# A written-out order of 1,498 words for a hash-attention and MLP kernel: PSUM banks dealt as the score tiles are made, and the order remade from unit 3's scores on

## The chip, the cores and the metric

One core of one Trainium2 chip. The metric is device time in microseconds (us) of one execution. The kernel before took 294.7 us, the median of three runs (295.97, 294.70 and 294.19).

## What is computed

Attention over 4 batches, 8 heads, 768 positions of 64 numbers, in which a query sees only the keys of its own hash bucket; then a layer norm and a two-matrix MLP with a residual over rows of 512.

```python
q_bits = (einsum('bhsd,dk->bhsk', q, proj) > 0)      # 6 bits for a query, the same for a key
q_bucket = sum(q_bits * powers, axis=-1)
mask = q_bucket[:, :, :, None] == k_bucket[:, :, None, :]
scores = where(mask, scale * matmul(q, k.transpose(0, 1, 3, 2)), -1e9)
attn = softmax(scores)
x = matmul(attn, v).transpose(0, 2, 1, 3).reshape(B, S, H * D)
xn = (x - mean) / sqrt(var + 1e-06) * g_ln
out = x + maximum(xn @ w_ch1, 0.0) @ w_ch2
```

## The kernel before, in words

The work is cut into 12 units of 256 query rows, three for each batch (unit u belongs to batch u // 3), and each unit into two halves g of four heads.

**A list of words sets the order.** ORDER (line 16) holds 1,498 words such as `S.t.7.1.0`: an operation, an engine (t TensorE, v VectorE, a ScalarE, p GpSimd, s the DMA queue of SyncE), and its place. Line 911 runs through the list and calls for each word the function of that name, so each engine does its words in the order in which they stand, and waits in line where an operand isn't there. Nothing reorders them later. The words that the prediction speaks of:

- `S.t.u.g.k` (S_, line 596) is a score word: 12 matmuls for keys k of unit u, half g, in three rounds (hash bits, then the two halves of q and k), on four groups of 32 rows at once. Six words, k = 0 to 5, make six tiles of two banks each: words 0 to 2 make tiles a = 0, words 3 to 5 tiles a = 1. With the first word of three come the tiles p = 0 and 1, with the second p = 2 and the rest of p = 1, with the third the rest of p = 0 and 2. So p = 1 is complete after the words k = 0 and 1 (3 and 4), p = 0 after k = 0 and 2 (3 and 5), p = 2 after k = 1 and 2 (4 and 5).
- `E.a.u.g.a.p` (line 622) is the exponential of one such tile on ScalarE, 1024 numbers a partition; it gives the tile's banks back. `A.t.u.g.a.p` (line 627) multiplies it with V into a tile acc, which `na.v` (line 644) reads.
- `sv.a.u.t` (line 672) is ScalarE's sum of squares of a row block for the layer norm, `ce.v.u.t` (line 685) centres and scales it, `fl.s.u.t` (line 704) turns it by a transposing DMA.
- The MLP's first matrix is `F.t.u.p` with `R` as its relu (units 0 to 3 and 11), or for units 4 to 10 seven products `M.t.u.p.h` (line 776) whose partial sums are copied by `V` (line 796) and added by `U` (line 807) or `Q` (line 811). The second matrix is `P.t.u.k` (line 872) in seven products, and `Y.v` adds each to x. `O.s` (line 890) writes x out.
- `mw.s` and `mr.s` (line 570) write the hash bits of a batch's half to DRAM and read them back as rows of G, which the score words take.

**Banks are dealt by a table.** PSUM has six banks for score and acc tiles, in three pairs (tag `pp`), and two for everything else (tag `f`). Each tile takes, when it is made, the next figure of a string in SLOTS (line 167) as the number of its slot; line 267 does it:

```python
def ps(name, shape, tag, dt=F32):
    if name not in made:
        n = taken.get(tag, 0)
        taken[tag] = n + 1
        tags[name] = f"{tag}_{SLOTS[tag][n]}"
        made[name] = psum.tile(shape, dt, name=name, tag=tags[name])
    return made[name]
```

A tile in a slot waits until the last reader of the tile before it in that slot is done. SBUF tiles (tags E, X, x and others) are dealt in the same way by `sb` (line 256).

Of the kernel before, what the change touches and what calls it, by code (L numbers as in the profile page):

```python
# [81 lines left out]
Y.v.3.7 hm.t.3.0 bt.v.3.0 S.t.6.0.3 N.a.6.0.1 S.t.6.0.4 E.a.6.0.1.1 bs.v.4.1 bs.v.4.3 bs.v.4.2 S.t.6.0.5
mr.s.2.1.3 E.a.6.0.1.2 O.s.2.0 sp.t.2.0 sc.v.2.0 mr.s.2.1.2 LX.s.3.1.0 mr.s.2.1.1 P.t.3.4 Y.v.3.4 M.t.4.1.0
V.v.4.1.0 E.a.6.0.1.0 M.t.4.2.0 U.v.4.1.0 mw.s.3.0 S.t.6.1.0 O.s.3.0 N.a.6.1.0 w1s.v.4.0 M.t.4.6.0 sv.a.5.1
M.t.4.5.0 V.v.4.5.0 S.t.6.1.1 bs.v.4.4 V.a.4.6.0 M.t.4.7.0 U.v.4.4.0 M.t.4.3.0 sv.a.5.0 E.a.6.1.0.1 S.t.6.1.2
E.a.6.1.0.0 U.v.4.2.0 M.t.4.4.0 Q.v.4.0 rs.p.5 A.t.6.0.1.1 tu.v.3.1.0.0 ce.v.5.1 M.t.4.1.1 A.t.6.0.1.2
A.t.6.0.0.1 M.t.4.2.1 V.a.4.1.1 U.v.4.1.1 E.a.6.1.0.2 tu.v.3.1.0.3 A.t.6.0.0.0 M.t.4.6.1 V.a.4.6.1 lv.s.3.0.2
lv.s.3.4.0 LX.s.3.1.1 O.s.3.3 lv.s.3.0.1 A.t.6.0.1.0 A.t.6.0.0.2 na.v.6.0 O.s.3.2 M.t.4.5.1 ru.v.4.1 fl.s.5.1
M.t.4.7.1 S.t.6.1.4 S.t.6.1.3 ce.v.5.0 V.a.4.5.1 U.v.4.4.1 M.t.4.3.1 U.v.4.2.1 N.a.6.1.1 E.a.6.1.1.1 S.t.6.1.5
E.a.6.1.1.0 M.t.4.4.1 Q.v.4.1 mr.s.3.0.0 P.t.4.1 E.a.6.1.1.2 ru.v.4.4 ru.v.4.2 ss.v.4.1 P.t.4.2 fl.s.5.0  # L90
lv.s.3.0.3 S.t.7.0.0 N.a.7.0.0 S.t.7.0.1 S.t.7.0.2 E.a.7.0.0.1 E.a.7.0.0.0 Y.v.4.2 Y.v.4.1 P.t.4.5 O.s.2.2
ss.v.4.2 O.s.3.1 ss.v.4.4 ss.v.4.3 bs.v.5.1 Y.v.4.5 P.t.4.6 tu.v.3.1.1.0 A.t.6.1.0.0 Y.v.4.6 A.t.6.1.0.1
A.t.6.1.0.2 nb.v.6.0 E.a.7.0.0.2 P.t.4.3 Y.v.4.3 lv.s.3.4.3 P.t.4.7 A.t.6.1.1.0 A.t.6.1.1.2 sp.t.2.4
A.t.6.1.1.1 sc.a.2.4 Y.v.4.7 P.t.4.4 M.t.5.1.0 tu.v.3.1.1.3 bs.v.5.2 na.v.6.1 mr.s.3.0.1 Y.v.4.4 S.t.7.0.3
tu.v.3.1.0.2 lv.s.3.4.2 bs.v.5.3 V.a.5.1.0 N.a.7.0.1 tu.v.3.1.0.1 S.t.7.0.4 E.a.7.0.1.1 M.t.5.2.0 U.v.5.1.0
S.t.7.0.5 E.a.7.0.1.2 E.a.7.0.1.0 M.t.5.6.0 M.t.5.5.0 S.t.7.1.0 V.v.5.6.0 N.a.7.1.0 M.t.5.7.0 S.t.7.1.2
V.a.5.5.0 S.t.7.1.1 nb.v.6.1 mn.p.6 E.a.7.1.0.0 sv.a.6.1 lv.s.3.4.1 O.s.4.1 bs.v.5.4 M.t.5.3.0 U.v.5.4.0
M.t.5.4.0 O.s.2.3 mr.s.3.0.3 Q.a.5.0 A.t.7.0.0.1 A.t.7.0.1.2 U.v.5.2.0 A.t.7.0.1.1 M.t.5.1.1 E.a.7.1.0.1
M.t.5.2.1 on.p.3 A.t.7.0.0.0 A.t.7.0.0.2 E.a.7.1.0.2 tu.v.3.1.1.1 A.t.7.0.1.0 V.v.5.1.1 M.t.5.6.1 U.v.5.1.1
na.v.7.0 M.t.5.5.1 O.s.4.0 S.t.7.1.3 tu.v.3.1.1.2 V.a.5.6.1 M.t.5.7.1 V.a.5.5.1 ru.a.5.1 M.t.5.3.1 U.v.5.4.1  # L100
N.a.7.1.1 sv.a.6.0 S.t.7.1.4 S.t.7.1.5 E.a.7.1.1.1 E.a.7.1.1.0 E.a.7.1.1.2 U.v.5.2.1 rs.p.6 M.t.5.4.1 ru.v.5.4
Q.v.5.1 ru.v.5.2 hm.t.3.1 P.t.5.2 S.t.8.0.0 N.a.8.0.0 S.t.8.0.1 ss.v.5.1 E.a.8.0.0.1 ce.v.6.1 ss.v.5.3
bt.v.3.1 fl.s.6.1 S.t.8.0.2 E.a.8.0.0.0 E.a.8.0.0.2 nb.v.7.0 P.t.5.1 cv.a.3.4.0 A.t.7.1.0.1 A.t.7.1.1.2
Y.v.5.2 Y.v.5.1 ss.v.5.2 ce.v.6.0 A.t.7.1.0.2 A.t.7.1.0.0 A.t.7.1.1.1 A.t.7.1.1.0 na.v.7.1 nb.v.7.1 mn.p.7
P.t.5.6 Y.v.5.6 S.t.8.0.3 N.a.8.0.1 S.t.8.0.4 E.a.8.0.1.1 S.t.8.0.5 ss.v.5.4 E.a.8.0.1.0 P.t.5.5 P.t.5.7
bs.v.6.3 E.a.8.0.1.2 Y.v.5.5 P.t.5.3 su.v.3.0 S.t.8.1.0 N.a.8.1.0 sv.a.7.1 S.t.8.1.1 S.t.8.1.2 E.a.8.1.0.2
Y.v.5.3 sp.t.3.0 Y.v.5.7 sc.v.3.0 P.t.5.4 sv.a.7.0 rs.p.7 fl.s.6.0 M.t.6.1.0 mw.s.3.1 mr.s.3.1.2 cv.v.3.0.0
A.t.8.0.1.2 A.t.8.0.0.0 Y.v.5.4 V.v.6.1.0 O.s.4.3 A.t.8.0.0.1 bs.v.6.1 M.t.6.2.0 bs.v.6.2 E.a.8.1.0.1
# [63 lines left out]
    X="012302312031201001",  # L172
# [14 lines left out]
    x="012301320132",  # L187
    xnT="010101010101",
)

@with_exitstack
def kernel(
    ctx: ExitStack,
# [750 lines left out]
```

## Time and profile before

| | |
|---|---|
| runs shown | 295.97, 294.70, 294.19 us; median 294.70 |
| the profiled execution, its own time | 293.72 us |
| its span in the trace | 292.0 us (1.7 us lie around it) |
| granted TensorE clock | 1.00 |
| TensorE matmuls busy | 280.4 us, 96% of the span |
| VectorE, ScalarE, GpSimd busy | 244.8, 228.9, 32.9 us |
| exponentials on ScalarE | 144 of 1.11 us, 152.2 us |

The trace names a tile without its numbers (sc for every score tile). "Releaser" is what ended the idle time before an instruction. A matmul's bar reaches some 0.17 us beyond the start of the next one, since matmuls are pipelined, so short waits do not show as idle time; the distance from the start of one word to the start of the next shows them.

### The profile page before, as it was taken

The numbers are of one execution on the slowest core, as the hardware profiler recorded it, in microseconds if no ns is written. First come the engines' busy times: TensorE is split into PE (matmuls) and PEld (weight loads), VectorE is DVE, ScalarE is ACT, GpSimd is POOL, SyncE is SP. The second block draws the span as 40 slices with busy tenths as digits, with TensorE's granted clock in tenths as the row PEclk, the third lists the DMA queues.
The fourth block names the chain that finished last, engine by engine and source line by source line (L and its number), as shares of the span: only waits on it lengthen the run. The fifth ranks groups of instructions, "written<-read, shape, count | busy, mean of one in ns | idle before, by whom it ended". The sixth has DMA issues, their size and how long they took to land.

```text
span 292.0 us, 11314 instructions
## 1 busy us (share of the span) xinstructions
PE 280.4 (96%) x4924; PEld 228.0 (78%) x4927; DVE 244.8 (84%) x587; ACT 228.9 (78%) x285; POOL 32.9 (11%) x83
## 2 busy tenths in 40 slices
PE   8998999999999999999998999899999999999993
PEld 5777767558887886877886878698788789998882
DVE  5758899899998989898997899797997997998552
ACT  4889999999999859879847989898897896664240
POOL 4560500110003002001000102000101011010000
PEclk9999999999999999999999999999999999999999
DMA  6999999268752560444942012500042202003233
GB/s 205 362 293 270 217 278 173 58 203 225 203 159 75 135 225 2 111 146 106 205 140 60 4 38 57 114 11 2 12 101 56 57 3 55 24 0 56 53 93 91
DMA packets 31059, 34.15 MB, mean 117 GB/s; under 512 B 15521, under 2 KB 27809, under 8 KB 31010
## 3 DMA queue, kind: packets, MB, share of 16 engines
q1 hardware_dynamic: 25938, 28.72, 35.4%
q0 software_dynamic: 4224, 4.19, 8.7%
q8 instruction: 38, 0.62, 0.9%
q10 hardware_dynamic: 848, 0.53, 0.7%
q14 instruction: 11, 0.09, 0.1%
HBM read 27.86 MB, written 6.88 MB: 119 GB/s over the span
## 4 chain that ended last, share of the span: by engine, by line
PE 84%; DVE 7%; ACT 6%; issue 1%; DVEq 0%; ACTq 0%
PE sc L606 17%; PE X L880 12%; PE acc L634 11%; PE f L725 10%; PE Ma L791 7%; PE Yb L880 6%; ACT E L623 4%; PE Ya L880 3%; PE Me L791 3%; PE hp L550 3%; PE hf L418 3%; PE f L828 2%; PE Mb L791 2%; PE warm L388 1%; DVE T L329 1%
## 5 line engine op out<-in xcount | busy, mean ns | idle before, releaser
L623 ACT ACTIVATE E<-sc,bias_sb 128x1024 bf16<-128x1024 f32 x144 | 152.2, 1112 | 17.8 <-PE sc L606 17.2
L606 PE MATMUL sc<-qb,kb 32*128 32x256 bf16 x1152 | 52.4, 267 | 0.0
L606 PE MATMUL sc<-G 6*128 6x256 bf16 (+1 forms) x576 | 43.0, 272 | 3.2 <-ACT E L623 3.1
L634 PE MATMUL acc<-vaug,E 128*128 128x65 bf16 x1152 | 43.1, 193 | 0.4 <-ACT E L623 0.4
L634 PEld LDWEIGHTS <-E 128*128 128x128 bf16 x1152 | 40.5, 97 | 2.1 <-issue 1.0
L725 PE MATMUL f<-xnT,w_sb 128*128 128x256 bf16 x320 | 38.8, 273 | 0.4 <-ACT hb L733 0.2
L880 PEld LDWEIGHTS <-hb 128*128 128x128 bf16 x352 | 33.0, 98 | 7.3 <-issue 3.1
L725 PEld LDWEIGHTS <-w_sb 128*128 128x128 bf16 x320 | 30.2, 98 | 5.4 <-issue 2.1
L606 PEld LDWEIGHTS <-kb 32*128 32x128 bf16 x1152 | 30.6, 93 | 1.2
L606 PEld LDWEIGHTS <-G 6*128 6x128 bf16 (+1 forms) x576 | 17.4, 91 | 17.2 <-issue 12.4
L733 ACT ACTIVATE hb<-f 128x512 bf16<-128x512 f32 x33 | 19.6, 599 | 13.5 <-PE f L725 10.5
L880 PEld LDWEIGHTS <-S 128*128 128x128 bf16 x264 | 25.2, 98 | 4.3 <-issue 1.1
L329 DVE STREAM_TRANSPOSE T<-X 128x384 f32<-128x384 f32 (+2 forms) x52 | 26.6, 539 | 0.0
L885 DVE TENSOR_TENSOR x<-X,x 128x256 f32<-128x256 f32 x44 | 18.3, 418 | 5.8 <-PE X L880 5.6
L880 PE MATMUL Yb<-w_sb,S 128*128 128x256 bf16 x176 | 22.8, 273 | 0.0
L791 PEld LDWEIGHTS <-w_sb 128*128 128x128 bf16 x336 | 20.2, 97 | 3.0 <-issue 2.8
L880 PE MATMUL X<-wt,hb 128*128 128x256 bf16 x168 | 21.8, 273 | 0.0
L791 PEld LDWEIGHTS <-Wx 128*128 128x128 bf16 x336 | 19.6, 98 | 2.3 <-issue 2.1
L646 DVE SCALAR_TENSOR_TENSOR y<-vsB,acc 128x520 f32<-128x520 f32 x24 | 16.6, 690 | 5.0 <-PE acc L634 4.8
L669 POOL TENSOR_TENSOR rw<-rw 128x2 f32<-128x2 f32 x9 | 2.1, 237 | 139.1 <-DVE x L659 139.1
L791 PE MATMUL Ma<-bs,Wx 128*128 128x128 bf16 x192 | 14.7, 219 | 0.0
L659 DVE SCALAR_TENSOR_TENSOR x<-y,rc 128x256 f32<-128x256 f32 x36 | 13.9, 422 | 0.6
(134 smaller groups left out, 441.4 us busy)
## 6 DMA issues: line engine op xcount, KB each, us to landing
out_dram<-x SPq DMA_DIRECT2D x45, 128.0 KB
X<-in_k_dram SPq DMA_DIRECT2D x7, 768.0 KB
vn<-in_v_dram SPq DMA_DIRECT2D x24, 192.0 KB
X<-in_q_dram SPq DMA_DIRECT2D x6, 768.0 KB
w_sb<-in_moe_w_ch_dram POOLq DMA_DIRECT2D x8, 512.0 KB, 12.5
vn<-in_v_dram SPq DMA_DIRECT2D x2, 768.0 KB
X<-in_q_dram SPq DMA_DIRECT2D x2, 512.0 KB
Bd<-B SPq DMA_DIRECT2D x6, 96.0 KB
```

Of the source, the lines that this page charges most:

```text
L329: nc.vector.transpose(d[:, j], s[:, j, kj0 : kj0 + n])
L418: nc.tensor.matmul(hf(g, t, kp)[:, :256], pfull[:, j], tp(g, t, kp)[:, j], start=(j == 0), stop=(j == 1))
L606: m = nc.tensor.matmul(sc(u, g, a, p)[:, bank, 256 * half : 256 * half + 256], lh, rh, start=(rep == 0), stop=(rep == 2), skip_group_check ...
L623: nc.scalar.activation(Ep(u, g, a, p), sc(u, g, a, p), AF.Exp, scale=EXP_SCALE, bias=bias_sb)
L634: nc.tensor.matmul(acc[:, qt, (D + 1) * i : (D + 1) * (i + 1)], Ep(u, g, a, p)[:, bank, 256 * half + P * qt : 256 * half + P * qt + P], va ...
L646: nc.vector.scalar_tensor_tensor(yt(u, g), vs, EPS_ROW, made[f"acc{u}_{g}"][:, :, :A], op0=AOP.mult, op1=AOP.add,)
L659: nc.vector.scalar_tensor_tensor(xo[:, t], a[:, t, :, 0:D], 1.0, rc[:, t].to_broadcast([P, 4, D]), op0=AOP.mult, op1=AOP.mult, accum_out=r ...
L725: nc.tensor.matmul(f1[:, n].rearrange("p (t x) -> p t x", t=2), w1_sb[:, dt, P * nt : P * nt + P], xnT(u)[:, :, dt], start=(dt == 0), stop ...
L733: nc.scalar.activation(hb(u)[:, 2 * p : 2 * p + 2], f1, AF.Relu)
L791: nc.tensor.matmul(m[:, n], lh(kt)[:, P * nt : P * nt + P], rh[:, kt], start=(first and n == 0 and kt == 0), stop=(kt == 1), skip_group_ch ...
L880: nc.tensor.matmul(f2, lh[:, n], rh[:, n], start=(first and n == 0), stop=(n == 7), skip_group_check=True)
L885: nc.vector.tensor_tensor(x, made[f"{prod(u, k)}{u}"], x, op=AOP.add)
```

## The change

The first 299 words stay. From the scores of unit 3 on the list is another: the same work in another sequence, with 44 words on another engine (ScalarE or VectorE; seen over all, 304 words stand on ScalarE before and 300 after, 454 and 458 on VectorE; TensorE and SyncE have the same words, 550 and 144). Five strings of SLOTS change with it: pp, f, E, X and x. No function changes, and no arithmetic. "Measured times of the squares" is a note on how the new list was made (the durations of sv); it has no line in the code.

One line of the list and the string of the score banks, before and after:

```diff
-A.t.6.1.1.1 sc.a.2.4 Y.v.4.7 P.t.4.4 M.t.5.1.0 tu.v.3.1.1.3 bs.v.5.2 na.v.6.1 mr.s.3.0.1 Y.v.4.4 S.t.7.0.3
+A.t.6.1.1.0 S.t.7.0.3 sp.t.2.4 A.t.6.1.0.1 sc.a.2.4 cv.a.3.0.0 N.a.7.0.1 Y.v.4.7 P.t.4.4 bs.v.5.1 tu.v.3.1.1.0
...
-    pp="012120212021102012012012010120120201021021021012021002010212102012102121012011022021210021010201201020120102102120102101200210201210202110210212012021120101201201202102021",
+    pp="012120212021102012012012010120120201021021021010202112010212012102120101210212101021201210201210211020120102102120121020121201021010210212012101021021012021021022101201021",
```

**The first place: ScalarE at the scores of unit 7** (E7_010 is the exponential of unit 7, half 0, a = 1, p = 0; V550 the copy of a product of unit 5; a cast to vaug is V of batch 3). Before:

```order
L623 ACTIVATE E7_011_3716<-sc7_011_3684,bias_sb_66 128x1024
L623 ACTIVATE E7_012_3741<-sc7_012_3703,bias_sb_66 128x1024
L623 ACTIVATE E7_010_3743<-sc7_010_3681,bias_sb_66 128x1024
L800 COPY V550_3800<-Me50_3753 128x512
L623 ACTIVATE E7_100_3820<-sc7_100_3762,bias_sb_66 128x1024
```

After:

```order
L623 ACTIVATE E7_010_3748<-sc7_010_3649,bias_sb_66 128x1024
L623 ACTIVATE E7_012_3750<-sc7_012_3700,bias_sb_66 128x1024
L800 COPY V550_3761<-Me50_3752 128x512
L623 ACTIVATE E7_011_3764<-sc7_011_3652,bias_sb_66 128x1024
L498 CAST vaug3_3208<-vn30_2840 128x12x64
L623 ACTIVATE E7_100_3821<-sc7_100_3767,bias_sb_66 128x1024
```

Tile p = 0 was the third exponential and is the first. On TensorE the words of a = 1 went k = 3, 4, 5 and go 3, 5, 4; between the last of them and `S.t.7.1.0` stand the products M.5.6.0 and M.5.5.0, as before. The tile sc7_100 of that word takes the slot of sc7_010, and sc7_101 that of sc7_012, before and after alike.

**The second place: ScalarE between the scores of unit 8 and of unit 9.** Before:

```order
L800 COPY V660_4432<-Ma60_4334 128x512
L800 COPY V650_4479<-Me60_4434 128x512
L623 ACTIVATE E8_111_4509<-sc8_111_4446,bias_sb_66 128x1024
L623 ACTIVATE E8_110_4512<-sc8_110_4457,bias_sb_66 128x1024
L623 ACTIVATE E8_112_4522<-sc8_112_4443,bias_sb_66 128x1024
L813 ACTIVATE hb6_4425<-Ma60_4334 128x4x128
L623 ACTIVATE E9_000_4564<-sc9_000_4524,bias_sb_66 128x1024
```

After:

```order
L800 COPY V660_4423<-Ma60_4328 128x512
L674 ACTIVATE xc7_4364,rw7_4148<-x7_4147,rw7_4148 128x512
L623 ACTIVATE E8_111_4481<-sc8_111_4434,bias_sb_66 128x1024
L623 ACTIVATE E8_110_4495<-sc8_110_4431,bias_sb_66 128x1024
L623 ACTIVATE E8_112_4497<-sc8_112_4447,bias_sb_66 128x1024
L800 COPY V611_4565<-Ma61_4534 128x512
L623 ACTIVATE E9_000_4576<-sc9_000_4519,bias_sb_66 128x1024
```

The three exponentials keep their order; what moves here are the slots. Figures 123 to 128 of the string pp (counted from 0) belong to this place. Before they read 2, 1, 0 for sc8_112, sc8_111, sc8_110 and 2, 0, 1 for sc9_000, sc9_001, sc9_002: sc9_000 takes the slot of the third exponential, sc9_001 that of the second. After they read 2, 0, 1 for sc8_110, sc8_111, sc8_112 and 0, 2, 1 for the tiles of unit 9: sc9_000 takes the slot of the first exponential, sc9_001 that of the second, and sc9_002, which a later word makes, that of the third. The copy V650 has gone to VectorE, and a sum of squares of unit 7 stands in its place.

**The third place: the last rows of the DMA queue of SyncE** (x11 is the last unit's x; 64x512 and 64x256 are its last pieces). Before:

```order
L899 DMA out_0_dram<-x10_5539 32x1024 x2
L899 DMA out_0_dram<-x9_5001 32x1024
L897 DMA out_0_dram<-x11_6054 64x512
L899 DMA out_0_dram<-x9_5001 32x1024
L897 DMA out_0_dram<-x11_6054 64x256 x2
```

After:

```order
L899 DMA out_0_dram<-x9_4993 32x1024 x3
L899 DMA out_0_dram<-x8_4572 32x1024
L899 DMA out_0_dram<-x10_5553 32x1024
L899 DMA out_0_dram<-x9_4993 32x1024
L899 DMA out_0_dram<-x10_5553 32x1024 x3
L897 DMA out_0_dram<-x11_6119 64x512
L897 DMA out_0_dram<-x11_6119 64x256 x2
```

A piece of unit 9 stood between two pieces of unit 11 and now stands ahead of all of them.

Two more moves are spoken of below. `ce.v.4.0` and `ce.v.4.1` come later on VectorE, behind `na.v.5.0`, six or seven words of TensorE later, and the transposes of unit 4 stand on SyncE right ahead of the hash rows `mr.s.2.1`, which the first score word of unit 6, half 1 takes. And from the first score word of unit 3 on, the score words stand in 51 groups without another TensorE word between them, where they stood in 49; 18 of the groups are a single word, where 14 were.

More of the change, by code (lines that the diff above doesn't have):

```diff
@@ new lines @@
+tu.v.3.0.1.3 na.v.5.0 S.t.5.1.3 N.a.5.1.1 S.t.5.1.4 E.a.5.1.1.1 mw.s.2.1 ce.v.4.0 lv.s.3.0.0 ce.v.4.1
+tu.v.3.0.0.2 tu.v.3.0.1.0 O.s.2.2 Y.v.3.2 ss.v.3.1 ss.v.3.3 S.t.5.1.5 E.a.5.1.1.0 P.t.3.1 ss.v.3.2 Y.v.3.1
+P.t.3.5 ss.v.3.4 tu.v.3.0.0.3 P.t.3.6 E.a.5.1.1.2 S.t.6.0.0 N.a.6.0.0 S.t.6.0.1 S.t.6.0.2 E.a.6.0.0.0 Y.v.3.5
+P.t.3.3 E.a.6.0.0.2 E.a.6.0.0.1 Y.v.3.6 tu.v.3.0.0.0 P.t.3.7 lv.s.3.4.0 fl.s.4.0 fl.s.4.1 A.t.5.1.0.2
+A.t.5.1.0.1 A.t.5.1.0.0 A.t.5.1.1.0 A.t.5.1.1.2 A.t.5.1.1.1 mr.s.2.1.2 mr.s.2.1.1 LX.s.3.1.1 nb.v.5.0
@@ new lines @@
+U.v.7.2.0 E.a.9.1.1.1 M.t.7.1.1 ce.v.8.0 Q.v.7.0 S.t.10.0.0 M.t.7.2.1 N.a.10.0.0 S.t.10.0.1 E.a.10.0.0.1
+V.v.7.1.1 ce.v.8.1 U.v.7.1.1 S.t.10.0.2 M.t.7.6.1 ru.v.7.1 M.t.7.5.1 A.t.9.1.0.0 V.a.7.5.1 V.v.7.6.1
+A.t.9.1.1.2 M.t.7.7.1 M.t.7.3.1 U.v.7.4.1 E.a.10.0.0.2 E.a.10.0.0.0 A.t.9.1.0.1 A.t.9.1.1.1 U.v.7.2.1
+A.t.9.1.0.2 M.t.7.4.1 ru.v.7.4 sp.t.3.4 ru.v.7.2 A.t.9.1.1.0 O.s.6.1 sc.v.3.4 Q.a.7.1 na.v.9.1 S.t.10.1.0
+ss.v.7.1 N.a.10.1.0 fl.s.8.0 fl.s.8.1 P.t.7.2 S.t.10.1.2 Y.v.7.2 O.s.6.2 E.a.10.1.0.0 S.t.10.1.1 E.a.10.1.0.1
@@ new lines @@
+sv.a.11.1 sv.a.11.0 ru.v.9.2 ss.v.9.1 ss.v.9.2 M.t.10.6.1 M.t.9.4.1 M.t.10.1.0 P.t.9.1 Q.a.9.1 P.t.9.2
+V.a.10.1.0 M.t.10.6.0 O.s.8.0 rs.p.11 ss.v.9.4 bs.v.10.4 Y.v.9.2 V.a.10.6.1 Y.v.9.1 ss.v.9.3 M.t.10.7.1
+U.v.10.4.1 P.t.9.5 Y.v.9.5 ce.v.11.0 P.t.9.6 Y.v.9.6 P.t.9.3 ce.v.11.1 Y.v.9.3 V.a.10.6.0 V.a.10.5.0
+M.t.10.7.0 U.v.10.4.0 O.s.8.1 M.t.10.4.1 fl.s.11.0 M.t.10.2.0 U.v.10.2.1 U.v.10.1.0 M.t.10.3.0 U.v.10.2.0
+P.t.9.7 fl.s.11.1 Y.v.9.7 M.t.10.2.1 U.v.10.1.1 ru.v.10.1 ru.a.10.4 Q.a.10.1 M.t.10.4.0 ru.v.10.2 P.t.9.4
@@ L159 @@
+ss.v.11.3.1 P.t.11.3 Y.v.11.6 P.t.11.7 Y.v.11.3 O.a.11.0.1 O.s.11.0.0 Y.v.11.7 O.a.11.1.1.1 O.s.11.1.0.1
+P.t.11.4 Y.v.11.7.1.0 Y.v.11.4 O.s.11.1.0.0 O.a.11.1.1.0
 """
@@ L186 @@
     vsum="000",
-    x="012301320132",
+    x="012301230123",
     xnT="010101010101",
```

213 lines of the change are left out of this document (98 added, 115 removed).

## The prediction, written before the changed kernel was run

> **What bounds the kernel now.** The page first, for the engines and the chain that ended last.
>
> ```profile
> PE 280.4 (96%) x4924; PEld 228.0 (78%) x4927; DVE 244.8 (84%) x587; ACT 228.9 (78%) x285; POOL 32.9 (11%) x83
> PE 84%; DVE 7%; ACT 6%; issue 1%; DVEq 0%; ACTq 0%
> ```
>
> TensorE is busy for 96% of the span and carries 84% of the chain. The order stays the same up to unit 3's scores (about 58 us), so I asked for the busy time by stretches from there.
>
> ```profile
> 60.00:100.00 40.00, 39.94 (x628) 31.18 (x627) 36.56 (x80) 37.26 (x46) 3.40 (x8) 1.00 0.59 161
> 100.00:140.00 40.00, 39.65 (x697) 31.80 (x696) 36.24 (x87) 33.16 (x43) 3.01 (x8) 1.00 0.43 126
> 140.00:160.00 20.00, 18.73 (x359) 15.59 (x356) 17.96 (x46) 13.24 (x16) 0.68 (x4) 1.00 0.57 129
> 180.00:200.00 20.00, 18.85 (x392) 16.15 (x391) 17.10 (x38) 17.25 (x22) 0.90 (x2) 1.00 0.24 54
> 280.00:292.00 12.00, 7.38 (x68) 6.36 (x65) 6.14 (x16) 1.34 (x3) 0.00 (x0) 1.00 0.25 77
> ```
>
> The first figure after the length is TensorE. It loses 1.27 us in one stretch, 1.15 in another, next to nothing in the rest, and 4.62 at the end. The granted clock is 1.00 throughout. So there is little to win: the words themselves fill the time. The waits say what the two losses are.
>
> ```profile
> PE sc L606 <- ACT E L623: 3.1, 5, 1.3
> ```
>
> Score words wait for exponentials: a tile cannot be made until the tile before it in its slot has been read. The timeline shows the two large cases, TensorE and ScalarE.
>
> ```profile
> 155.18 0.29 PE L606 MATMUL sc<-G 6*128 6x256 bf16 x4
> 155.62 0.62 PE L791 MATMUL Ma<-bs,Wx 128*128 128x128 bf16 x8
> 156.10 0.61 PE L791 MATMUL Me<-bs,Wx 128*128 128x128 bf16 x8
> 157.97 0.29 PE L606 MATMUL sc<-G 6*128 6x256 bf16 x4 [1.27 <-ACT E L623]
> 154.80 3.12 ACT L623 ACTIVATE E<-sc,bias_sb 128x1024 bf16<-128x1024 f32 x3 [0.20 <-PE sc L606]
> 185.73 0.61 PE L791 MATMUL Ma<-bs,w_sb 128*128 128x128 bf16 x8
> 187.43 0.29 PE L606 MATMUL sc<-G 6*128 6x256 bf16 x4 [1.09 <-ACT E L623]
> 184.25 3.12 ACT L623 ACTIVATE E<-sc,bias_sb 128x1024 bf16<-128x1024 f32 x3 [0.22 <-PE sc L606]
> ```
>
> At 157.97 and 187.43 a score word starts within 0.1 us of the end of the third exponential in a row (154.80 + 3.12 = 157.92; 184.25 + 3.12 = 187.37). Three take 3.12 us, so one more costs 1.04, and the last ends 0.1 later than that.
>
> **Unit 7 (the first place).** A product before scores starts 0.55 us ahead of them, a score word alone takes 0.44 (155.18 to 155.62), a product 0.48. From 156.10 to 157.97 are 1.87 us, so 1.32 are lost. Now the first word of unit 7, half 1 needs the exponentials p = 0 and p = 2, which were the third and second and are the first and second. Count from the start of the score word k = 5. Its exponential starts at 0.44 + 0.17 = 0.61. The product M.5.2.0 and the word k = 4 end at 0.44 + 0.55 + 0.44 = 1.43; the second exponential follows the first at 1.65 and ends at 1.65 + 1.11 = 2.76. TensorE, after two products, wants the next scores at 1.43 + 0.48 + 0.55 = 2.46. That leaves a wait of 0.35. The third exponential now stands behind a copy, and one V cast more stands ahead of the next; for `S.t.7.1.2` and the first A word I leave 0.1 us. **Gain 1.32 - 0.45 = 0.9.**
>
> **Unit 9 (the second place).** From 185.73 to 187.43 are 1.70, less 0.55: 1.15 lost. sc9_000 waited for the third exponential; now the later of its two tiles waits for the second, 1.04 earlier, and what needs the third comes one product and one word later. But a sum of squares, not a copy, now stands ahead of the three.
>
> ```profile
> L674 ACT ACTIVATE xc<-x,rw 128x512 bf16<-128x512 f32 x18 | 12.9, 718 | 0.8 <-DVE vsum L507 0.5 <-PE sc L606 0.3
> L800 ACT COPY V<-Ma 128x512 f32<-128x512 f32 x13 | 7.6, 585 | 6.4 <-PE Ma L791 3.0 <-DVE hb L809 1.8 <-DVE x L885 1.2
> ```
>
> That is 0.72 against 0.59, with its own reading of the sum 0.1 behind it: some 0.2 us later. **Gain 1.04 - 0.2 = 0.8.**
>
> **Two smaller waits of the same kind.** The chain in order of time leaves TensorE for ScalarE before 116.27, and the timeline shows what that costs, and a like wait at 265.98.
>
> ```profile
> 114.33 0.89 ACT xc L674 x3
> 115.22 1.01 ACT E L623
> 116.27 1.62 PE acc L634 x48
> ```
>
> ```profile
> 114.10 1.92 PE L725 MATMUL f<-xnT,w_sb 128*128 128x256 bf16 x16
> 264.70 1.04 PE L880 MATMUL X<-wt,hb 128*128 128x256 bf16 x8
> 265.98 0.61 PE L791 MATMUL Mae<-bs,w_sb 128*128 128x128 bf16 x8 [0.24 <-DVE hb L809]
> 218.76 0.87 PE X L880 x8
> ```
>
> Eight products of 256 columns take 0.87. From 114.10 to 116.27 two such words have 2.17 and not 1.74, from 264.70 to 265.98 one has 1.28: 0.4 lost in each. At 116.27 the acc tile of unit 5 waits for an exponential that stands behind two sums of squares of unit 4; in the new list acc5_0 takes the slot of a tile read sooner. At 265.98 the product M.10.4.0 waits for VectorE's adds; another product, M.10.2.1, and its 0.48 us now stand ahead of it. Each may keep all of it or lose all. **I take 0.7 of 0.8.**
>
> **The end (the third place).** The last add ends at 287.42 + 0.42 = 287.84:
>
> ```profile
> 286.74 0.84 SPq L899 DMA_DIRECT2D out_dram<-x  x1
> 287.42 0.42 DVE L885 TENSOR_TENSOR x<-Yc,x 128x256 f32<-128x256 f32 x1
> 287.68 1.20 SPq L897 DMA_DIRECT2D out_dram<-x  x2
> ```
>
> The queue issues a piece of unit 9 until 287.58 and then two of unit 11, 0.6 each, so the last starts at 288.28 and not at 287.84. With unit 9's piece ahead of both, it starts with the add's end. **Gain 0.4**, certain as long as the last product ends last.
>
> **What it costs.** A group of score words has a price at its edges:
>
> ```profile
> 215.16 0.98 PE Ya L880 x8
> 216.14 0.77 PE sc L606 x24
> 219.63 1.10 PE sc L606 x36
> ```
>
> Two words take 0.77 and three 1.10, so a word is 0.33 and the group 0.11 on top; the product next to it takes 0.98 and not 0.87. So 0.22 a group, and 51 groups for 49: **0.44 lost.** Nothing else on TensorE changes in number. The 44 words that change engine are costed at nothing: VectorE gets four more in all and ScalarE four fewer, and the shortest and the longest of those that move,
>
> ```profile
> L823 DVE TENSOR_SCALAR hb<-hb 128x1024 bf16<-128x1024 bf16 x15 | 6.1, 422 | 0.2
> L340 DVE CAST kb<-T 128x1536 bf16<-128x1536 f32 x3 | 2.9, 951 | 0.0
> ```
>
> make that 1.7 to 3.8 us for VectorE, under its idle time (3.4 of 40 in its fullest stretch above, and 230 us to spread them over). Without that cover they are the price.
>
> **New waits** cannot be read from a trace of before. Bounds: none at all, or two as large as the two largest now (1.27 + 1.09 = 2.4). The nearest rows are the other waits among products and scores, of which there are many, all short:
>
> ```profile
> 207.85 0.61 PE L791 MATMUL Ma<-bs,w_sb 128*128 128x128 bf16 x8 [0.17 <-DVE hb L809]
> ```
>
> I take two of these, **0.3 lost**, because the units 4 to 8 still put the same products between scores and the same three exponentials behind them.
>
> Sum: -0.9 - 0.8 - 0.7 - 0.4 + 0.44 + 0.3 = -2.06, say -2.1. The profiled execution took 293.72 us (292.0 and 1.7 around it), so it would take 291.6. The median of the runs is 1.0 above that execution, so the forecast is **292.6 us**, 0.7% faster.
>
> **The rivals.**
>
> 1. *The waits go altogether.* All waits of score words for exponentials go (3.1 by the waits), the 0.8 of the two smaller ones and the 0.4 of the end, and no new ones come: -4.3 + 0.44 = -3.9, that is 290.8 for a run. For it: the slots now follow the order of reading. Against: at unit 7 the sum above still has 0.35. Chance 0.15.
> 2. *The waits only move.* New waits take 2.4, as bounded above: 294.7, no change. For it: a list of 1,200 words that shifts 44 between engines meets many queues, and at unit 7 two casts of V now stand between the exponentials; it decides where such a cast and one more exponential outlast two products. Against: the sums at the two largest places leave 0.35 each. Chance 0.22.
> 3. *The hash rows of unit 6 come late: slower.* `ce.v.4` now stands behind `na.v.5.0`, and SyncE's queue behind `ce.v.4`: the transposes of unit 4 and then the rows of G.
>
> ```profile
> 116.93 1.23 SPq L705 DMA_TRANSPOSE xnT<-xc  x1
> 119.35 2.44 SPq L705 DMA_TRANSPOSE xnT<-xc  x1
> 126.14 0.68 SPq L571 DMA_DIRECT2D G<-Bd  x1
> 134.31 0.29 PE L606 MATMUL sc<-G 6*128 6x256 bf16 x4
> SPq L571 <- DMA Bd<-B: 7.4, 2, 5.1
> ```
>
> The last row was issued by 126.8 and used at 134.31, a slack of 7.5 less the flight. Six or seven words later at 0.44 to 0.87 are some 4 us, which uses half of it. The queue has waited up to 5.1 for such rows' source. If the lateness passes the slack by that, the scores, all that follows and the end move by 5.1: 292.6 + 5.1 = 297.7. Against it: the slack. Chance 0.05.
>
> 4. *VectorE sets the pace: slower.* Then the waits of TensorE give nothing back, and four more words on VectorE cost 1.7 to 3.8 us, 2.8 in the middle: 294.7 + 2.8 = 297.5. It decides once VectorE has more work between two products that wait for its adds than TensorE has words between them. For it: VectorE is busy for 36.56 of 40 us in a stretch. Against: TensorE has 39.94 there, and its words of eight products follow each other at 0.87. Chance 0.03. A rule of the Trainium skill would have it so: Perfetto Trace Analysis, Identifying the Most-Contended Engine, says that matmul busy time does not tell how near TensorE is to its peak and that the share of weight loads does, and that share is 78%, under VectorE's 84%; the row of 0.87 speaks against it here, and no run has tested it.
>
> The forecast itself has 0.55, from 290.6 to 294.4 (the new waits from none to 2.4, the smaller ones kept or lost). That the change doesn't do what it says can be ruled out, since the strings and the list stand in the code.
>
> **The numbers.** About 1% (2.9 us) is what a measurement of this kernel can tell from no change; faster by more is under 291.8, slower by more over 297.6. Faster: nearly all of rival 1 (0.14) and some two fifths of the forecast's own range (0.20). Slower: most of rival 3 and half of rival 4, 0.06. Same: 0.60. The range, 289.6 to 296.0, leaves out rivals 3 and 4 and the far end of rival 1.
>
> **What would show it.** Right: no wait of a score word above 0.5 us in the waits; at the first score word of unit 9 the wait ends with the second of three exponentials; the last issue on SyncE starts within 0.1 of the last add's end; the stretches after 60 us lose under 1.5 us together. Wrong: waits of 1 us at other score words or products (rival 2), idle time ended by a DMA of G near 133 (rival 3), or products of 256 columns that take other than 0.87.

## The result, and the profile after

The changed kernel takes **292.54 us** (median of 5, 291.59 to 292.74) where the kernel before took 294.57 beside it (median of 5): ratio 0.9932, 95% interval 0.9902 to 0.9961. In a second turn it took 291.77 against 294.08: 0.9914 (0.9884 to 0.9944). So it is 0.7 to 0.9% faster, which is under the 1% that I said can be told from no change, though both intervals lie below 1.

The profiled execution took 292.62 us by its own time, with a span of 290.9. The page of after, engines and chain:

```profile
PE 281.8 (97%) x4927; PEld 228.6 (79%) x4927; DVE 246.7 (85%) x591; ACT 224.7 (77%) x281; POOL 34.5 (12%) x83
PE 88%; DVE 8%; ACT 2%; issue 1%; DVEq 0%; ACTq 0%
```

TensorE carries 88% of the chain and no longer 84%, ScalarE 2% and not 6%. The stretches of after (TensorE is the first figure behind the length):

```profile
60.00:100.00 40.00, 39.98 (x652) 30.82 (x652) 37.33 (x81) 32.33 (x41) 3.35 (x6) 1.00 0.70 172
100.00:140.00 40.00, 39.93 (x691) 32.19 (x692) 37.14 (x89) 34.05 (x43) 3.33 (x10) 1.00 0.50 150
140.00:160.00 20.00, 19.95 (x378) 16.54 (x375) 19.13 (x48) 16.18 (x20) 0.61 (x3) 1.00 0.30 72
180.00:200.00 20.00, 19.78 (x404) 16.96 (x401) 17.83 (x44) 18.28 (x24) 1.34 (x4) 1.00 0.30 53
```

The 1.27 us of 140 to 160 are 0.05, the 1.15 of 180 to 200 are 0.22. The waits of after:

```profile
PE sc L606 <- ACT E L623: 0.8, 3, 0.3
```

It was 3.1 in five waits, the longest 1.3; now none is above 0.3. The timeline of after at the two places, TensorE and ScalarE, shows why:

```profile
155.46 2.12 ACT L623 ACTIVATE E<-sc,bias_sb 128x1024 bf16<-128x1024 f32 x2 [0.91 <-PE sc L606]
156.82 0.61 PE L791 MATMUL Me<-bs,Wx 128*128 128x128 bf16 x8
157.36 0.54 PE L606 MATMUL sc<-G 6*128 6x256 bf16 x4
158.00 1.12 ACT L623 ACTIVATE E<-sc,bias_sb 128x1024 bf16<-128x1024 f32 x1
...
183.62 3.16 ACT L623 ACTIVATE E<-sc,bias_sb 128x1024 bf16<-128x1024 f32 x3
185.34 0.61 PE L791 MATMUL Ma<-bs,w_sb 128*128 128x128 bf16 x8 [0.22 <-DVE hb L809]
185.88 0.29 PE L606 MATMUL sc<-G 6*128 6x256 bf16 x4
```

At unit 7 the score word starts 0.54 behind the product, as a word without a wait does. Only its four hash matmuls take 0.54 and not 0.29: the first two write a tile whose slot is free, the other two wait for the second exponential, which ends at 157.58. At unit 9 nothing waits: the second of the three exponentials ends at 183.62 + 2 x 1.05 = 185.7, and the word starts at 185.88.

For what follows I cut the execution at two instants that every trace has: the start of the first score word of the program, and the end of the last product. These are their rows, of before and of after:

```profile
7.52 0.29 PE L606 MATMUL sc<-G 32*128 32x256 bf16 x4
286.34 1.04 PE L880 MATMUL Yc<-wt,hb 128*128 128x256 bf16 x8
```

```profile
8.20 0.29 PE L606 MATMUL sc<-G 32*128 32x256 bf16 x4
284.83 1.04 PE L880 MATMUL Yc<-wt,hb 128*128 128x256 bf16 x8
```

| profiled execution | head, to the first score word | middle, to the last product's end | tail, to the end of the span | span |
|---|---|---|---|---|
| before | 7.52 | 279.86 | 4.61 | 292.0 |
| after | 8.20 | 277.67 | 5.04 | 290.9 |
| difference | +0.68 | -2.19 | +0.43 | -1.1 |

The head is the same list in both kernels; over the fourteen profiles of this study it is 7.2 to 8.4, whatever the kernel, so it is noise. The middle is where the words are, and repeats to 0.1 (277.67 and 277.74 in two profiles of the changed kernel). The tail went the wrong way.

### The profile page after: what moved, and what is told of

It reads as the page before. It is cut to its first block, busy times and chain, and to the rows that moved or that the text cites. A ratio compares the mean times of both kernels' runs of the same rounds, so it can differ in the third digit from the quotient of the medians.

```text
span 290.9 us, 11317 instructions
## 1 busy us (share of the span) xinstructions
PE 281.8 (97%) x4927; PEld 228.6 (79%) x4927; DVE 246.7 (85%) x591; ACT 224.7 (77%) x281; POOL 34.5 (12%) x83
## 4 chain that ended last, share of the span: by engine, by line
PE 88%; DVE 8%; ACT 2%; issue 1%; DVEq 0%; ACTq 0%
PE sc L606 18%; PE X L880 13%; PE acc L634 12%; PE f L725 11%; PE Ma L791 7%; PE Yb L880 7%; PE Me L791 3%; PE Ya L880 3%; PE hp L550 3%; PE hf L418 3%; PE f L828 2%; PE Mb L791 2%; ACT E L623 2%; PE warm L388 1%; DVE T L329 1%; DVE hb L809 1%
## 5 line engine op out<-in xcount | busy, mean ns | idle before, releaser
L606 PE MATMUL sc<-G 6*128 6x256 bf16 (+1 forms) x576 | 43.6, 273 | 0.9 <-ACT E L623 0.8
L669 POOL TENSOR_TENSOR rw<-rw 128x2 f32<-128x2 f32 x9 | 2.9, 321 | 130.9 <-DVE x L659 130.9
```

What stands on the lines that cost most here:

```text
L606: m = nc.tensor.matmul(sc(u, g, a, p)[:, bank, 256 * half : 256 * half + 256], lh, rh, start=(rep == 0), stop=(rep == 2), skip_group_check ...
```

## The experiments

Theory A is the prediction's: TensorE sets the pace, the slot of a tile decides which exponential it waits for, and removing those waits is the gain. Theory B, with a form of its own in each run: the gain comes from something else in the new list, or waits only move.

| run | median, us | ratio to before, 95% interval | middle | tail |
|---|---|---|---|---|
| e1_slots9 | 292.59 | 0.9924 (0.9896 to 0.9952) | 278.87 | 4.64 |
| e2_slots7 | 293.07 | 0.9945 (0.9923 to 0.9967) | 278.88 | 4.64 |
| e3_slots79_end | 292.11 | 0.9918 (0.9883 to 0.9952) | 277.89 | 4.28 |
| e4_undo79 | 296.29 | 1.0058 (1.0025 to 1.0091) | 280.08 | 4.93 |
| e5_after | 291.77 | 0.9914 (0.9884 to 0.9944) | 277.74 | 4.99 |
| e6_best | 292.13 | 0.9919 (0.9887 to 0.9950) | 277.75 | 4.28 |
| e7_groups | 294.60 | 1.0007 (0.9988 to 1.0025) | 280.59 | 4.26 |
| e8_vload | 293.83 | 0.9986 (0.9962 to 1.0010) | 280.45 | 4.27 |
| e9_vload_idle | 291.31 | 0.9901 (0.9865 to 0.9938) | 277.92 | 4.26 |
| e10_best2 | 292.47 | 0.9941 (0.9917 to 0.9964) | 278.21 | 4.28 |
| e11_undo9 | 293.10 | 0.9961 (0.9935 to 0.9988) | 279.89 | 5.06 |
| e12_shift | 291.87 | 0.9924 (0.9906 to 0.9943) | 278.12 | 4.39 |

Medians of 6 to 12 executions, each against before in the same turn on the same chip (294.33 beside e1 to e4, 294.08 beside e5 to e8, 293.97 beside e9 to e11, 294.06 beside e12). Differences of a few tenths are read from the middle and the tail, not from the medians.

**The slots alone, one place at a time.**

```diff
-    pp="012120212021102012012012010120120201021021021012021002010212102012102121012011022021210021010201201020120102102120102101200210201210202110210212012021120101201201202102021",
+    pp="012120212021102012012012010120120201021021021012021002010212102012102121012011022021210021010201201020120102102120102101200210102120101220120121021012210202102102101201012",
```

> The list of before, and one relabelling of its score banks from unit 9 on (figures 1 and 2 of the string pp changed for each other from sc9_000 on), so that sc9_000 takes the slot of the first of the three exponentials of unit 8 and sc9_002 that of the third. Theory A (TensorE sets the pace, and the slot of a tile decides which exponential it waits for): the first score word of unit 9 starts 0.1 us after the second exponential and not after the third, its wait falls from 1.15 us to 0.35, the word that makes sc9_002 waits 0.2, and the run takes 294.57 - 0.8 = 293.8 us with the profile's span 291.2. Theory B (the slots only pass the wait on; the gain needs the new sequence): product M.6.2.1, whose bank ScalarE gives back behind the same three exponentials, waits the 0.8 instead, and the run stays at 294.5.

The same exchange of figures from sc7_100 on:

```diff
-    pp="012120212021102012012012010120120201021021021012021002010212102012102121012011022021210021010201201020120102102120102101200210201210202110210212012021120101201201202102021",
+    pp="012120212021102012012012010120120201021021021012021002010212102012102121012011022021210021010201201020120201201210201202100120102120101220120121021012210202102102101201012",
```

> The list of before, and one relabelling of its score banks from sc7_100 on (figures 1 and 2 changed for each other), so that sc7_100 takes the slot of the first of the three exponentials of unit 7, half 0 and sc7_102 that of the last. Theory A: the first score word of unit 7, half 1 starts with the end of the second exponential, its wait of 1.32 us falls to 0.35, the word that makes sc7_102 waits 0.2, and the run takes 293.8 us. Theory B: product M.5.3.0, whose partial sum ScalarE copies behind the third exponential, takes the wait over, and the run stays at 294.5.

Each shortens the middle by 1.0 (279.86 to 278.87 and 278.88), 0.2 more than expected, and no product took the wait over: theory A. The medians fell by more, 1.7 and 1.3 (from 294.33 to 292.59 and 293.07). Part of that is the mix of executions: six of the 26 of before in that turn took 295.9 to 296.3, five of them at a mean granted clock of 0.993, and none of e1 or e2 did. The timeline of e1_slots9 at unit 9:

```profile
183.93 3.12 ACT L623 ACTIVATE E<-sc,bias_sb 128x1024 bf16<-128x1024 f32 x3 [0.21 <-PE sc L606]
185.41 0.61 PE L791 MATMUL Ma<-bs,w_sb 128*128 128x128 bf16 x8
185.95 0.43 PE L606 MATMUL sc<-G 6*128 6x256 bf16 x4
186.53 0.62 PE L791 MATMUL Ma<-xnT,w_sb 128*128 128x128 bf16 x8
```

What a word loses, here and below, is the distance from its start to the start of the next word, less the shortest such distance between two words of these kinds (0.54 from a product to scores, 0.43 from a score word to a product). The score word here starts at once, since its first tile is free, and loses 0.15 inside (its hash matmuls take 0.43 and not 0.29), until the second exponential ends at 186.0. The wait at S.7.1.0 in e2_slots7 is 0.34 by the same measure.

**Both, and the end.**

```diff
-O.s.9.3 O.s.11.0.0 O.s.9.2 Y.v.11.7.1.0 P.t.11.4 O.s.11.1.0.1 Y.v.11.4 O.s.11.1.0.0 O.a.11.1.1.0
+O.s.9.3 O.s.9.2 O.s.11.0.0 Y.v.11.7.1.0 P.t.11.4 O.s.11.1.0.1 Y.v.11.4 O.s.11.1.0.0 O.a.11.1.1.0
```

> The list of before with both relabellings (sc7_100 on and sc9_000 on) and one word moved: the piece of unit 9 that stood between two pieces of the last unit in the queue of SyncE now stands ahead of them. Nothing else of the change. Theory A: the two waits give 0.8 each and the end 0.4, so 294.57 - 2.0 = 292.6 us, as much as the whole change gave (292.54), with 90 figures and one word of 1,498. Theory B: only the end gives, 294.2.

The middle is 1.97 shorter, the tail 0.33, the median 292.11 where 292.6 was expected. The whole change has 2.19 and -0.43. So two relabellings and one word give as much as the change; the rest of the new list, 1,200 words and 44 changes of engine, is worth 0.2 in the middle, all its gains and costs together.

**The change without the two slots.**

```diff
-    pp="012120212021102012012012010120120201021021021010202112010212012102120101210212101021201210201210211020120102102120121020121201021010210212012101021021012021021022101201021",
+    pp="012120212021102012012012010120120201021021021010202112010212012102120101210212101021201210201210211020120201201210212010212102210202102101201020210210201210210211020120210",
```

> The changed kernel, its list as it stands, with the score banks relabelled so that sc7_100 again takes the slot of the last of the three exponentials of unit 7, half 0, and sc9_000 that of the last of unit 8. Theory A: the first score word of unit 7, half 1 waits for the third exponential, which now stands behind a copy of 0.5, 1.3 us more than in the changed kernel, and that of unit 9 0.8 more, so 292.54 + 2.1 = 294.6 us. Theory B: the new sequence carries the gain, so it stays under 293.2.

```profile
157.13 1.12 ACT L623 ACTIVATE E<-sc,bias_sb 128x1024 bf16<-128x1024 f32 x1
158.30 0.29 PE L606 MATMUL sc<-G 6*128 6x256 bf16 x4 [1.74 <-ACT E L623]
```

At unit 7 the word waits for the third exponential (157.13 + 1.12 = 158.25) and loses 1.81; at unit 9 it loses 0.98. The middle is 2.4 longer than in the changed kernel and 0.2 longer than in the kernel before: without the two slots the change has no gain. That is theory A. The median of 296.29 is above the 294.6 expected: ten of its twelve executions had a mean granted clock of 0.984 to 0.992 and took 295.6 to 298.0; the two at 0.997 and 0.998 took 294.29 and 294.05. The same with unit 9 alone:

```diff
-    pp="012120212021102012012012010120120201021021021010202112010212012102120101210212101021201210201210211020120102102120121020121201021010210212012101021021012021021022101201021",
+    pp="012120212021102012012012010120120201021021021010202112010212012102120101210212101021201210201210211020120102102120121020121201120101201202102010120120102120120122010210120",
```

> The changed kernel with the score banks relabelled from sc9_000 on alone (figures 0 and 1 changed for each other), so that sc9_000 takes the slot of the last of the three exponentials of unit 8. Theory A: the first score word of unit 9 waits for the third exponential, 1.0 us, and the time is 0.8 above the changed kernel's 291.8 to 292.5, so 292.6 to 293.3. Theory B (the time of the kernel with both tiles undone, 296.3, is not the two waits but something that the relabelling of unit 9 sets off): 294 or more.

Median 293.10, as theory A has it; the score word of unit 9 loses 0.98. Its middle is 2.2 longer than that of after: 0.98 is this wait, and 1.3 lie ahead of the scores of unit 3, where the clock fell in its profile (below).

**The changed kernel again, and two further changes to the list of before.** The lines of the list are cut to the words that matter from here on.

> The changed kernel itself once more, on the chip of the three kernels beside it. Theory A (two relabelled tiles carry the gain, the rest of the change gives about as much as it costs): 0.7% under before, 292.2 to 292.6 us, and no faster than the list of before with the two relabellings and the end word (292.11, ratio 0.9918). Theory B (the new sequence carries a gain of its own): over 1 us under that kernel's ratio, 291.0.

291.77, 0.4 under the 292.2 to 292.6 expected, but 0.9914 of before against 0.9918 for e3: it repeats, and its middle of 277.74 against 277.89 says that neither list is ahead by anything that counts.

```diff
-mn.p.4 sv.a.4.1 sv.a.4.0 S.t.5.1.1 S.t.5.1.2 rs.p.4 E.a.5.1.0.2
+mn.p.4 sv.a.4.1 S.t.5.1.1 S.t.5.1.2 E.a.5.1.0.2 sv.a.4.0 rs.p.4
...
-U.v.10.2.1 U.v.10.2.0 M.t.10.2.0 P.t.9.7 U.v.10.1.0 Y.v.9.7
+U.v.10.2.0 M.t.10.2.0 P.t.9.7 U.v.10.1.0 U.v.10.2.1 Y.v.9.7
```

> The list of before with the two relabellings and the end word, and two more moves. The second sum of squares of unit 4 (with the rsqrt word on GpSimd behind it) goes behind the exponential that acc5_0 waits for; and the add U.v.10.2.1 goes behind U.v.10.2.0 and U.v.10.1.0 on VectorE, since product M.10.4.0 waits for the second. Theory A (TensorE sets the pace, every wait of its words is worth its length): the 0.41 at 115 us and the 0.41 and 0.16 at 264 us go, 0.9 us together, so 292.1 - 0.9 = 291.2 us, 1.05% under before, and faster than the changed kernel. Theory B (the adds wait for ScalarE's relu and the next product for the add moved back): 0.4 only, 291.7.

Theory A failed here. The 0.41 at 115 us and the 0.57 at 264 us went, and 0.14 were gained of 0.9: in their place P.3.5 waits 0.21, P.9.4 0.26 for an add that the moved one has pushed back, and P.10.2 0.38 for ScalarE's Q:

```profile
265.50 0.72 PE L880 MATMUL Ya<-w_sb,hb 128*128 128x256 bf16 x5 [0.21 <-ACT hb L813]
```

```diff
-M.t.5.6.0 M.t.5.5.0 S.t.7.1.0 V.v.5.6.0 N.a.7.1.0 M.t.5.7.0 S.t.7.1.2
+M.t.5.6.0 M.t.5.5.0 V.v.5.6.0 M.t.5.7.0 S.t.7.1.0 N.a.7.1.0 S.t.7.1.2
...
-S.t.9.0.0 N.a.9.0.0 Q.a.6.0 M.t.6.1.1 CA.v.3.1.1 S.t.9.0.2
+M.t.6.1.1 S.t.9.0.0 N.a.9.0.0 Q.a.6.0 CA.v.3.1.1 S.t.9.0.2
```

> The list of before with the two relabellings and the end word, the second sum of squares of unit 4 behind the exponential that acc5_0 waits for, and two groups of score words fewer: M.5.7.0 ahead of S.7.1.0 and M.6.1.1 ahead of S.9.0.0, so 47 groups. Theory A: 0.2 a group and 0.2 of the square (0.41 gone, 0.21 come at 122), 0.6 us together, 291.5, 0.3 under the list with the relabellings alone and the changed kernel. Theory B (the score words then wait for the third exponential, and the products for their adds): no gain, 292.1.

Theory B: the middle is 0.3 longer than in e3. The score word had covered VectorE: without it M.5.7.0 waits for the copy of its partial sum and loses 0.48, M.6.1.1 loses 0.28.

```profile
156.64 0.69 DVE L802 COPY V<-Ma 128x512 f32<-128x512 f32 x1 [0.23 <-PE Ma L791]
157.38 0.61 PE L791 MATMUL Ma<-bs,Wx 128*128 128x128 bf16 x8 [0.32 <-DVE V L802]
```

**The price of a group.** One of ten such cuts:

```diff
-S.t.3.1.3 N.a.3.1.1 S.t.3.1.4 E.a.3.1.1.1 S.t.3.1.5 E.a.3.1.1.0 E.a.3.1.1.2 fl.s.2.1 fl.s.2.0 R.v.1.3 tu.v.2.0.1.3 P.t.1.2
+S.t.3.1.3 N.a.3.1.1 S.t.3.1.4 E.a.3.1.1.1 P.t.1.2 S.t.3.1.5 E.a.3.1.1.0 E.a.3.1.1.2 fl.s.2.1 fl.s.2.0 R.v.1.3 tu.v.2.0.1.3
```

> The list of before with the two relabellings and the end word, and ten groups of score words cut in two: in each the product that stood behind the last score word now stands ahead of it, so 59 groups where there were 49, and nothing else. Theory A (a group of score words has a price of 0.22 us at its edges): 10 x 0.22 = 2.2 us more, 294.3 us. Theory B (the 0.11 at each edge is the overlap of the records, not time): no change, 292.1 to 292.4, since none of the ten moved words comes to wait.

The middle is 2.70 longer than that of e3_slots79_end; of these 0.8 are new waits (0.29 at the largest), so ten groups cost 1.9, 0.19 each. Theory A. The cut above, uncut in e3_slots79_end and cut in e7_groups:

```profile
75.50 0.29 PE L606 MATMUL sc<-G 6*128 6x256 bf16 x4
...
76.60 1.05 PE L880 MATMUL Ya<-w_sb,hb 128*128 128x256 bf16 x8
77.48 0.60 PE L725 MATMUL f<-xnT,w_sb 128*128 128x256 bf16 x4
```

```profile
75.01 0.29 PE L606 MATMUL sc<-G 6*128 6x256 bf16 x4
...
75.78 1.05 PE L880 MATMUL Ya<-w_sb,hb 128*128 128x256 bf16 x8
76.76 0.29 PE L606 MATMUL sc<-G 6*128 6x256 bf16 x4
...
77.20 0.94 PE L725 MATMUL f<-xnT,w_sb 128*128 128x256 bf16 x7
```

The same three score words and one product take 77.48 - 75.50 = 1.98 in one piece and 77.20 - 75.01 = 2.19 in two.

**VectorE's cover.** A spare tile, and instructions on it that nothing waits for by data:

```diff
+    spare = pool.tile([P, 200], F32, name="spare")
+    def zz(eng, u):
+        if u == 2:
+            nc.gpsimd.memset(spare, 0.0)
+        for _ in range(2):
+            eng.tensor_tensor(spare, spare, spare, op=AOP.max)
...
-Y.v.5.4 V.v.6.1.0
+Y.v.5.4 zz.v.5 V.v.6.1.0
```

> The list of before with the two relabellings and the end word, and 18 instructions more on VectorE, in pairs behind the last add of units 2 to 10, on a spare tile that nothing else reads: 200 numbers a partition each, about 0.25 us, 4.5 us together, more than what the four words that the change gave to VectorE cost (1.7 to 3.8). Theory A (TensorE sets the pace, VectorE's words are hidden): under 0.4 us, 292.1 to 292.5. Rival 4 of the prediction (VectorE sets the pace): 4.5 us more, 296.6.

And one by one where VectorE was idle, one of 18 places:

```diff
-ss.v.2.3 Y.v.2.5 P.t.2.7
+ss.v.2.3 zz.v.18 Y.v.2.5 P.t.2.7
```

> The list of before with the two relabellings and the end word, and the same 18 instructions on the spare tile (0.36 us each in the profile of the run before), now one by one ahead of the VectorE words that had waited longest for TensorE (0.39 to 0.96 us of idle time each, between 90 and 274 us). Theory A, narrowed (TensorE sets the pace; an added VectorE word costs its length where a product waits for the next add behind it, and nothing in VectorE's idle time): under 0.5 us, 292.1 to 292.6. Rival (VectorE's total sets the pace, wherever the work stands): the same 1.7 us as in pairs, 293.8.

The instructions took 0.36 and not 0.25 us, 18 x 0.36 = 6.5. In pairs behind the last add of a unit they lengthened the middle by 2.56, neither 0.4 nor the whole. The waits of e8_vload show where it went. None of these three stands among the waits of e3_slots79_end:

```profile
PE Me L791 <- DVE hb L809: 0.9, 3, 0.3
PE Ma L791 <- DVE V L802: 0.6, 2, 0.4
PE f L725 <- DVE x L885: 0.5, 1, 0.5
```

Five of the nine pairs, ahead of copies and adds that the next products wait for, cost TensorE 0.5 to 0.7 each; the others next to nothing. In VectorE's idle time the same 18 cost 0.03 in the middle (277.92 against 277.89). The engines of e3_slots79_end and of e9_vload_idle, by their pages:

```profile
PE 281.1 (97%) x4927; PEld 228.1 (79%) x4927; DVE 244.6 (84%) x587; ACT 228.5 (79%) x285; POOL 32.9 (11%) x83
```

```profile
PE 280.7 (97%) x4924; PEld 227.9 (79%) x4927; DVE 249.9 (86%) x605; ACT 228.5 (79%) x285; POOL 33.2 (11%) x84
```

VectorE is busy for 5.3 us more and the time is no longer. So VectorE's total does not set the pace; what stands ahead of its adds does.

**The tail.** One of twelve places, and the spare tile as above, one instruction each:

```diff
-M.t.6.5.0 V.v.6.5.0 M.t.6.7.0
+M.t.6.5.0 zz.v.12 V.v.6.5.0 M.t.6.7.0
```

> The changed kernel, its list and slots as they stand, with 12 instructions more on VectorE (the spare tile of the two runs before, 0.36 us each), each ahead of a word for which VectorE waits 0.45 to 1.27 us. In the four profiles with the changed kernel's list the stretch from the end of the last product to the end of the span is 4.93 to 5.06 us, in those with the list of before and the end word 4.26 to 4.28, although the last issues start at the same distance from the last product. Theory A (VectorE runs 707 instructions there and not 699, so that a load of its code, an 8 KB packet of the queue for instructions, falls 1.5 us behind the last product, among the packets of the last piece): twelve instructions more move that load ahead of the last product, the last piece's packets end 2.4 us behind it and not 2.85, the stretch is 4.3 us, and the run takes 0.7 less than the changed kernel, 291.1 to 291.8, with 12 instructions more. Theory B (the order of the last rows in the queues makes the stretch): it stays at 5.0 and the run at 291.8 to 292.5.

The last issue on SyncE starts at 286.36 in after, 0.03 behind the last add's end (285.91 + 0.42) and 0.49 behind the last product's, exactly as in e3_slots79_end:

```profile
285.91 0.42 DVE L885 TENSOR_TENSOR x<-Yc,x 128x256 f32<-128x256 f32 x1
286.36 0.57 SPq L897 DMA_DIRECT2D out_dram<-x  x1
```

What differs is behind it. The DMA of after from 287.3 to 287.6, 1.4 to 1.7 us behind the last product, and from 288.35 to 288.8:

```profile
q1 hardware_dynamic: 41, 0.03, 32.0%
q10 hardware_dynamic: 14, 0.01, 14.8%
q14 instruction: 1, 0.01, 13.8%
```

```profile
DMA packets 8, 0.01 MB, mean 14 GB/s; under 512 B 2, under 2 KB 8, under 8 KB 8
```

A packet of the instruction queue (q14, which I take to carry a load of code) stands among the last pieces; 8 late packets of the output follow alone, the last of them 2.85 behind the last product, where 2.39 is the end in e3_slots79_end. That is 0.46 of the 0.76 by which the tail is longer than there; the other 0.3 lies behind the last packet, and no view shows what takes it. In e12_shift the same stretch behind the last product, 288.45 to 289.0, is empty:

```profile
DMA packets 0, 0.00 MB, mean 0 GB/s; under 512 B 0, under 2 KB 0, under 8 KB 0
```

Its code packet came 12.8 us ahead of the last product's end, its last output packet 2.37 behind it, and the tail is 4.39: 0.6 of the 0.7 came back, with the same last rows in the queues, so theory A holds for the mechanism. In e8_vload and e9_vload_idle, where VectorE runs 717 instructions, the packet stands 3.5 us ahead of the last product's end, and the tails are 4.27 and 4.26. That the code is VectorE's is read from this alone: the packet moves with the number of VectorE's instructions. The run did not get shorter (291.87 against 291.77): its middle is 0.38 longer, 0.24 of it ahead of the scores of unit 3, where none of the twelve stands.

No version is clearly faster than the changed kernel (e5): it and e3, e6, e9 and e12 lie between 291.3 and 292.1, and their intervals overlap.

## Why the prediction was right, point by point

The forecast, 292.6 us, met the median of 292.54, and the mechanism of its two largest terms is shown by e1 to e4. That it met the median to 0.1 is luck: the same kernel took 291.77 in the second turn, and the sum had errors that cancelled.

- **Unit 7, 0.9.** 1.34 went; 0.27 inside the word and 0.12 at `S.t.7.1.2` came. Measured 0.95.
- **Unit 9, 0.8.** 1.15 went, 0.14 more came at M.6.4.0 (0.38 where 0.24 was). Measured 1.0. Too small by 0.2: I counted the wait from the later of the word's two tiles, and half the word runs before it is needed. And the 0.2 that I charged for the square ahead of the three exponentials did not come: they start 0.42 ahead of the next score word (183.62 and 184.04), in e1_slots9, where a copy stands there, 0.37.
- **Two smaller waits, 0.7 of 0.8.** The 0.42 at 115 us is gone. At 264 us the 0.57 went (and 0.21 at P.9.1), and 0.60 came back between 258 and 263 us (0.22, 0.25, 0.13). Measured 0.6.
- **Groups, 0.44 lost.** 0.19 each by e7, so 0.4 for the two.
- **New waits, 0.3 lost.** All words after 57 us lost 9.15 us before and 6.63 after, each counted against the shortest distance between two words of its kinds; that is 2.5 less, and with the groups 2.1. The terms above sum to 2.55, so new waits elsewhere took little: the 0.3 was too much.
- **The end, 0.4: the failed step.** "Gain 0.4, certain as long as the last product ends last." The last issue did move from 0.97 to 0.49 behind the last product, and e3 shows what that is worth alone: 0.33. In the changed kernel the tail grew by 0.43 all the same. VectorE had 707 instructions, counted with its waits, where it had 699, and a load of code fell among the last packets, which e12 moved away. I had costed the 44 changes of engine by VectorE's idle time, and not by where its code is cut.
- **The 1.0 to the median** did not apply: the profiled execution of after took 292.62, as the median, and not 291.6. The middle was better than the sum by 0.5 (2.19 for 1.66), the tail worse by 0.8, the head later by 0.7.
- **The range of the forecast alone, 290.6 to 294.4,** does not come out of its own terms. With no new wait and all of the 0.8 the sum gives 292.6 - 0.3 - 0.1 = 292.2, with 2.4 of new waits and none of the 0.8 it gives 292.6 + 2.1 + 0.7 = 295.4. So the 0.20 for a faster end of this range had no ground, and the second turn's 291.77 lies below it.

The rivals. The waits did not go altogether (1): score words still wait 0.8 of the 3.1, and the time is 292.5 and 291.8, not 290.8. Waits that only move (2) did not decide here, but they did in e6 and e10, which tried to go on. Late hash rows (3) did not come: no wait of TensorE in after is ended by a DMA. VectorE as the pace (4) is refuted as a statement on its total by e9: the row of 0.87 was right against a ranking by the share of weight loads (79% against VectorE's 85%). The Trainium skill, Perfetto Trace Analysis, Identifying the Most-Contended Engine, has TensorE judged by that share and by its part of the peak arithmetic rate, and not by its busy time; here the busy time told more than the share. Yet the cover that I gave VectorE's moved words ("230 us to spread them over") was not the reason why they cost nothing; e8 shows that 0.7 us at the wrong place costs TensorE up to 0.66. Of what I said would show it right, all came but one: at unit 9 no wait is left that could end with the second exponential.

## What to carry to other kernels

Where a tile waits for its slot, ask which of several readers gives the slot back, and give the first tile made the slot that is read first: two exchanges of labels did as much here as a new order of 1,200 words. Once the engine that sets the pace is busy for 39.9 of 40 us, removing a small wait can merely uncover the one behind it (in e6 0.14 was left of 0.98), so cost a removed wait by what is late next. Work added to an engine that is not the bottleneck is priced by what stands behind it in line, not by that engine's idle time as a whole.

## What the runs showed of the hardware

**A load of code can delay data.** One 8 KB packet of the instruction queue, 0.66 us long, among the last output packets put the last of them from 2.39 to 2.85 us behind the last product; the three other profiles with that list have it too (2.75 to 2.81), and in e12, with twelve instructions more, the packet is 12.8 us ahead of the last product's end. The Trainium skill, Runtime: NRT & Kernel Launch, Instruction fetch mechanics, calls the cost of crossing from one block of code to the next mostly hidden; here it showed where the load met the last output, and the tails are 4.26 to 4.39 where it came 3.5 to 12.8 us ahead of the last product's end.

**The granted clock can halve in mid-run.** In the profile of e11 the rows from 28 to 36 us read 0.86 and 0.71, which is 0.14 x 4 + 0.29 x 4 = 1.7 us of full clock lost, and between 30.9 and 34.2 us it is 0.50:

```profile
24.00:28.00 4.00, 3.99 (x119) 3.53 (x118) 3.21 (x10) 3.95 (x6) 0.00 (x0) 1.00 1.14 286
28.00:32.00 4.00, 3.28 (x60) 2.47 (x60) 3.79 (x11) 3.92 (x4) 0.00 (x0) 0.86 1.19 199
32.00:36.00 4.00, 4.00 (x57) 2.84 (x52) 3.12 (x8) 2.88 (x4) 2.64 (x7) 0.71 0.68 193
30.90:34.20 3.30, 3.30 (x37) 2.29 (x36) 3.30 (x8) 2.73 (x4) 1.51 (x3) 0.50 0.72 116
```

The five executions of before in the first turn with a mean clock of 0.993 took 295.9 to 296.3 where the median was 294.3, and the four of e4 at 0.984 took 297.8 to 298.0, some 3.7 us more than its two at 0.997 and 0.998. One execution of before took 295.96 at 0.999, so a low clock is not the only thing that makes one long. The Trainium skill, TensorE: Matmul & The Clock Gate, Part 1, puts a fall to half rate behind an idle window of some 3.4 us. The half agrees with the 0.50; the idle window does not: TensorE was busy for 3.28 of the 4 us in which the clock fell, and for 3.31 of the same 4 us in the profile of before, where it did not fall. Why e4 had it in ten of twelve executions was not tried.
